# Sliding-window attention and a highway layer: scores in 64-column products, and three kinds of work moved between engines

## The chip, the cores and the metric

One core of a Trainium2 chip runs the whole kernel in one launch. The metric is the device time of one execution in microseconds, as the median of several runs. Engine names are those of the profile: PE is TensorE, with PEld its weight loads, DVE VectorE, ACT ScalarE, POOL GpSimd, and SP the queue that stores the results.

## The reference

Attention over 8 batches, 8 heads, 576 positions and head dimension 64, with a window of 128 positions backwards and a bias that falls linearly with distance, followed by a highway layer on the 4608 tokens of 512 features.

```python
scores = scale * np.matmul(q, k.transpose(0, 1, 3, 2))
bias = slopes[:, None, None] * (-np.abs(rel).astype(np.float32))[None, :, :]
mask = (rel >= 0) & (rel < window)            # rel = query position - key position
scores = np.where(mask, scores + bias[None], -1000000000.0)
attn = softmax(scores)                        # written out in the original
x = np.matmul(attn, v)                        # then heads side by side: (4608, 512)
H = np.maximum(x @ w_h, 0.0)
T = 1.0 / (1.0 + np.exp(-(x @ w_t + b_t)))
return (T * H + (1.0 - T) * x).astype(np.float32)
```

Inputs and output are float32; the kernel computes in bfloat16 with float32 sums.

## The kernel before

The attention is cut into 32 **units** (b, s, g): batch b, half s of the heads (four heads, whose two 32-wide halves of the head dimension stand on 32 partitions each), and half g of the sequence. The highway layer is cut into 36 **blocks** of 128 tokens: (b, 0) to (b, 3) for each batch, and (b, 4) on odd batches, which takes the first 64 tokens of two batches together.

Each kind of step has a letter. `L` loads q and k (line 105), v (111), weights and bias through POOL's queue, with a cast to bfloat16. `T` (line 156) transposes q or k of one half on DVE. `S` is set-up: relative positions on POOL and DVE, the masks `MT` by exp on ACT, the ones columns of v, the bias tile, `ident`. For each unit: `s` scores on PE (line 183), `e` exp on ACT (201), `m` the product with the mask `MT` on DVE (206), `p` the product with v on PE (214, 222 for the 64 first tokens, 234 for the neighbouring blocks), `n` division by the sum on DVE (247, 248). For each block: `x` transposes on PE (273), `c` copy on ACT (278), `h` the product with w_h (283), `u` relu minus x on DVE (288), `z` the product with w_t and the bias (296, 298), `a` tanh on ACT (302), `t` its scaling to a gate on ACT (306), `g` the product of gate and uu on DVE (310), `o` the sum with x on POOL (314), `d` the store on SP.

The order of all steps is a string written out by hand, `ORDER`; the digit behind s, p, x, h, z is the first of the PSUM banks it uses. All scores use banks 0 to 3, so the scores of a unit wait for the exp of the unit before; the other PE steps take turns on banks 4 to 7. Each engine takes its own instructions strictly in the order of the string and waits at each for the semaphores of what it needs. A load also waits for the load eight places before it.

A score step of a unit has 48 products, of 128 or 64 columns of weights (keys) by 128 or 64 queries, four at a time on four groups of 32 rows, and changes the shape of the tile inside the unit. The two 64-key neighbours of a block of 128 queries have products of their own:

```python
segs.append((P * i, P * i + D, P, 192 * o, 0, P))
...
segs.append((P * i + P, P * i + P, D, 192 * o + P, 0, D))
segs.append((P * i - D, P * i + D, D, 192 * o + P, D, D))
```

The memsets of set-up come last in it, in part 3, behind the relative positions, and the first loads of v stand before them in the string.

Of the kernel before, what the change touches and what calls it, by code (L numbers as in the profile page):

```python
# [9 lines left out]
P = 128  # L10
# [3 lines left out]

ORDER = (
    "LLLLLLSSSSLLLTLTLLs0LTLLLeLs0meTp4Lms0nep6LLnms0LeTp4LnLmx4x5cTp6Lz4nLs0atx6LTh4cez5uLTx"
    "4h7aLgcs0mcz5tuoeTz4Ldgp6aLmas0Lnp4eLh6noh7udx4Ts0cLx5tmh4cgex6uh5uLz7utmcs0LaTz6eLTp4oa"
    "ns0tdmp6ez4ngx5mp6cags0ntox4ez5TLdp6Tcos0anh4eLdTh5Lux6s0cuLz4meLTx5p6ams0cgh4tnoez5TLdp"
    "6utms0ah4egnoz5utLx6dmas0Lcx4gh5Teop6TLdcLs0tnLtz4egLup6oTh5aLdgtnos0z4uLdTx5x6Lch7maz5L"
    "cmeh4uLmp6aus0tnp4eggx6nh7ocp4touds0ndx6egz7gToh4amx5dcz7cTotz5aTLdp6aLgts0noh5euTx6Ldh4"  # L20
    "uz7cuz5matms0aTp6ex4nh5gcp6ms0uoz4neLdgx5mLp6aocs0nz4edmp6Tas0tnh4egx5oux6h7TcLdx4tz5uLc"
    "mtp6cmts0anh4egz5guop6Taodts0np4edmz6nx7map4cs0nx6gh7gToh4cez5uodup6Tdts0anx4x5mch6gz4uc"
    "oeTh5dx6uh7tas0ucz5gemz4op6tadgs0anoh5emdh4p6uttgus0onx5z4cdmtp6agox4nz5cdtgp6aotx4neh5d"
    "gh6oucz7udmz6ap4atx7nh6cgtx4gh5uocz7uodx6ah4gdcox5tz6gduz7oath4cdgaoz5uth4gdaotugdod"
# [3 lines left out]
def lists():  # L28

    units = [(b, s, g) for b in range(NB) for g in range(NG) for s in range(NS)]  # L30
    units[1], units[2] = units[2], units[1]
    blocks = []
    for b in range(NB):
        blocks += [(b, 0), (b, 1)] + ([(b, 4)] if b % 2 else []) + [(b, 2), (b, 3)]
    trs = [(b, s, w) for b in range(NB) for s in range(NS) for w in range(2)]
    loads = []
    for b in range(NB):
        for s in range(NS):
            loads += [("t", b, s, 0), ("t", b, s, 1)]
            if b < 2 or b % 2 == 0:  # L40
                n = 1 if b < 2 else 2
                loads += [("v", b, n, m) for m in ((0, 1, 2), (3, 4))[s]]
        if b == 0:
            loads += [("w", 0), ("w", 1), ("w", 2)]
    by = dict(L=loads, T=trs, S=list(range(4)))
    by.update({k: units for k in "sempn"})
    by.update({k: blocks for k in "xchuzatgod"})
    return by
# [3 lines left out]
def kernel(  # L52
# [10 lines left out]
    nc = tc.nc  # L63
# [17 lines left out]

    cp = ctx.enter_context(tc.tile_pool(name="const", bufs=1))
# [16 lines left out]
    REL = cp.tile([P, 448], F32, name="rel")  # L99
# [21 lines left out]
    def setup(part):  # L121
        if part == 0:
            rel = cp.tile([P, 448], I32, name="rel_i")
            far = cp.tile([P, 448], F32, name="far")
            for o in range(2):
                nc.gpsimd.iota(rel[:, 192 * o : 192 * o + 192], pattern=[[1, 192]], base=64,
                               channel_multiplier=-1)
                nc.gpsimd.iota(rel[0:D, 192 * o + P : 192 * o + 192], pattern=[[1, D]], base=0,
                               channel_multiplier=-1)
            nc.gpsimd.iota(rel[:, 384:448], pattern=[[1, D]], base=0, channel_multiplier=-1)  # L130
            nc.vector.tensor_copy(out=REL[:], in_=rel[:])
            nc.vector.tensor_scalar(out=far[:], in0=REL[:], scalar1=-63.5, scalar2=None,
                                    op0=ALU.add)
            nc.vector.tensor_tensor(out=far[:], in0=far[:], in1=far[:], op=ALU.mult)
            nc.vector.tensor_scalar(out=far[:], in0=far[:], scalar1=4096.0, scalar2=1.0e6,
                                    op0=ALU.is_gt, op1=ALU.mult)
            nc.vector.tensor_tensor(out=REL[:], in0=REL[:], in1=far[:], op=ALU.add)
        elif part < 3:
            s = part - 1
            for a in range(4):  # L140
                nc.scalar.activation(out=MT[s][:, a, :], in_=REL[:], func=ACTF.Exp,
                                     scale=-slopes[4 * s + a])
        else:
            for i in range(NB // 2):
                nc.vector.memset(VA[i][:, :, :, D:E], 1.0)
            nc.vector.memset(bT[:], 0.0)
            nc.vector.memset(ones0[:], 0.0)
            nc.vector.memset(ones0[0:1, :], 1.0)
            nc.vector.memset(ident[:], 1.0)
            nc.gpsimd.affine_select(  # L150
                out=ident[:], in_=ident[:], compare_op=ALU.is_equal, fill=0.0,
                base=0, pattern=[[1, P]], channel_multiplier=-1)
# [8 lines left out]
    PT, AV, X = {}, {}, {}  # L161

    def scores(b, s, g, bank):
        QT, KT = (TR[(4 * b + 2 * s + w) % NTR] for w in range(2))
        segs = []
        for o in range(2):
            i = 2 * g + o
            segs.append((P * i, P * i + D, P, 192 * o, 0, P))
        for o in range(2):
            i = 2 * g + o  # L170
            if i == 0:
                segs.append((P, P, P, P, 0, D))
            else:
                segs.append((P * i + P, P * i + P, D, 192 * o + P, 0, D))
                segs.append((P * i - D, P * i + D, D, 192 * o + P, D, D))
        if g == 0:
            segs.append((0, 0, P, 384, 0, D))
        first = True
        for k0, q0, m, col, row, n in segs:
            for e in range(2):  # L180
                for a in range(4):
                    rows = slice(32 * a, 32 * a + 32)
                    nc.tensor.matmul(  # L183
                        out=PS[row : row + m, bank + a, col : col + n],
                        lhsT=KT[rows, k0 : k0 + m, e], rhs=QT[rows, q0 : q0 + n, e],
                        start=first and e == 0, stop=e == 1, tile_position=(32 * a, row),
                        skip_group_check=True)
                first = False
# [5 lines left out]

    SB = {}
# [8 lines left out]
    def mask(b, s, g):  # L204
        p, w = PB[PT[b, s, g]], width(g)
        nc.vector.tensor_tensor(out=p[:, :, 0:w], in0=p[:, :, 0:w], in1=MT[s][:, :, 0:w],  # L206
                                op=ALU.mult)

    def pv(b, s, g, bank):
        AV[b, s, g] = bank  # L210
        me = PB[PT[b, s, g]]
        for o in range(2):
            for a in range(4):
                nc.tensor.matmul(  # L214
                    out=PS[:, bank + o, a * E : a * E + E], lhsT=me[:, a, 192 * o : 192 * o + P],
                    rhs=VA[b // 2][:, b % 2 * H + 4 * s + a, 2 * g + o, :],
                    start=a == 0, stop=False, skip_group_check=True)
        if g == 0 and b % 2:
            for a in range(4):
                for r in range(2):  # L220
                    at = 4 + a % 2
                    nc.tensor.matmul(
                        out=PS[r * D : (r + 1) * D, bank + a // 2, at * E : at * E + E],
                        lhsT=PB[PT[b - 1 + r, s, 0]][:, a, 384:448],
                        rhs=VA[b // 2][:, r * H + 4 * s + a, 0, :],
                        start=False, stop=True, tile_position=(0, r * D), skip_group_check=True)
        for o in range(2):
            i = 2 * g + o
            for a in range(4):
                for row, slot in ((0, i + 1), (D, i - 1)):  # L230
                    if slot < 0:
                        continue
                    orow = D - row
                    nc.tensor.matmul(  # L234
                        out=PS[orow : orow + D, bank + o, a * E : a * E + E],
                        lhsT=me[row : row + D, a, 192 * o + P : 192 * o + 192],
                        rhs=VA[b // 2][row : row + D, b % 2 * H + 4 * s + a, slot, :],
                        start=False, stop=True, tile_position=(row, orow), skip_group_check=True)
# [46 lines left out]

    def relu_sub(b, i):
        uu = UU[b, i] = ft.tile([P, DM], BF16, name="uu")
        nc.vector.scalar_tensor_tensor(  # L288
# [15 lines left out]
    def to_gate(b, i):  # L304
        tt = TT[b, i]
        nc.scalar.activation(out=tt[:], in_=tt[:], func=ACTF.Copy, bias=0.5, scale=0.5)  # L306

# [9 lines left out]
    def store(b, i):  # L317
# [5 lines left out]
        for r in range(2):  # L323
# [4 lines left out]
              h=mm_h, u=relu_sub, z=mm_z, a=tanh, t=to_gate, g=gate, o=add_x, d=store)  # L328
    by = lists()
    at = dict.fromkeys(by, 0)  # L330
    steps = iter("".join(ORDER))
    with tc.manual_schedule():
        for step in steps:
# [3 lines left out]
            if step in "spxhz":  # L337
                bank = int(next(steps))
                if step == "s":
                    SB[what] = bank  # L340
                what += (bank,)
            do[step](*what)
    assert all(at[i] == len(by[i]) for i in by)
# [29 lines left out]
```

## Time and profile before

| | us |
|---|---|
| median of 3 runs | 167.42 (167.25 to 167.76) |
| the profiled execution, its own time | 168.74 |
| its span, first to last instruction | 167.0 |
| PE, DVE, ACT, POOL busy | 134.0, 134.6, 111.2, 92.2 |
| granted TensorE clock, mean | 0.997 |

In the profile's lines, a group or a piece of the timeline names start, length, engine, line of the kernel, operation, tile written and read, shapes, how many instructions; in brackets behind it the idle time of the engine before, and what ended it. Busy times of neighbours on an engine overlap a little, so the time that an instruction really takes of its engine is the distance to the start of the next one where that does not wait.

### The profile page before, as it was taken

Reading aid. Unit: us, or ns where it says so; the run is one execution under the profiler, and the core shown is the slowest. Engines: PE = TensorE matmul, PEld = TensorE weight load, DVE = VectorE, ACT = ScalarE, POOL = GpSimd, SP = SyncE. Lnnn points to the kernel's source line nnn. Section 1 sums busy time; section 2 is a strip of 40 time slices with the busy share of each in tenths; the row PEclk is TensorE's granted clock in tenths of the full one; section 3 lists DMA queues with packets and bytes.
Section 4 is the critical chain, followed back from the end, with each engine's and each line's share of the span. In section 5 each row is a group of like instructions: output and inputs, shape, how many; then the busy total and the mean of one; then the engine's idle time right before and its main releaser. Section 6 shows DMA issues by size and latency. Waiting matters only on the chain.

```text
span 167.0 us, 6262 instructions
## 1 busy us (share of the span) xinstructions
PE 134.0 (80%) x2772; PEld 82.3 (49%) x2772; DVE 134.6 (81%) x213; ACT 111.2 (67%) x149; POOL 92.2 (55%) x106
## 2 busy tenths in 40 slices
PE   0002682999996988979999999999889999999960
PEld 0002561556654645646656465665556556655520
DVE  0357674869899899979999999999979978986560
ACT  3063642198598678669496977679766698687670
POOL 7609915759742593568965870825505233553752
PEclk9999999999999999999999999999999999999998
DMA  3977999999999999999999999296821113231443
GB/s 48 163 95 88 135 200 182 191 188 162 220 180 207 206 173 156 213 117 198 180 242 179 217 258 152 20 192 143 171 94 67 63 67 98 95 129 63 190 119 134
DMA packets 48235, 25.04 MB, mean 150 GB/s; under 512 B 38480, under 2 KB 39504, under 8 KB 48208
## 3 DMA queue, kind: packets, MB, share of 16 engines
q0 software_dynamic: 42960, 15.21, 83.9%
q1 hardware_dynamic: 5248, 9.44, 16.3%
q8 instruction: 21, 0.34, 0.8%
q14 instruction: 6, 0.05, 0.1%
HBM read 30.41 MB, written 9.44 MB: 239 GB/s over the span
## 4 chain that ended last, share of the span: by engine, by line
PE 49%; DVE 26%; DMA 10%; issue 7%; POOL 6%; POOLq 1%; DVEq 0%
PE ps L283 14%; PE ps L296 13%; PE ps L183 8%; DVE tr L156 7%; DMA ld<-in_q_dram 6%; DVE uu L288 5%; DVE p L206 5%; DVE x L248 5%; PE ps L273 4%; PE ps L234 4%; DMA va<-in_v_dram 4%; PE ps L298 3%; PE ps L214 3%; DVE uu L310 2%; POOL va L111 2%
## 5 line engine op out<-in xcount | busy, mean ns | idle before, releaser
L314 POOL TENSOR_TENSOR ot<-uu,x 128x512 f32<-128x512 bf16 x36 | 46.5, 1296 | 54.2 <-DVE uu L310 33.1
L201 ACT ACTIVATE p<-ps 128x1792 bf16<-128x1792 f32 (+1 forms) x32 | 49.9, 1560 | 19.0 <-PE ps L183 18.8
L183 PE MATMUL ps<-tr,tr 32*64 32x64 bf16 (+2 forms) x1536 | 26.8, 211 | 20.7 <-DVE tr L156 15.2
L156 DVE STREAM_TRANSPOSE tr<-ld 128x576 uint32<-128x576 uint32 x32 | 38.9, 1243 | 2.8 <-DMA ld<-in_q_dram 2.8
L296 PE MATMUL ps<-wT,xt 128*128 128x512 bf16 x144 | 38.0, 386 | 0.8 <-DVE uu L288 0.4
L283 PE MATMUL ps<-wH,xt 128*128 128x512 bf16 x144 | 36.2, 380 | 0.2 <-DVE x L248 0.2
L206 DVE TENSOR_TENSOR p<-p,mt 128x1792 bf16<-128x1792 bf16 (+1 forms) x32 | 32.2, 1013 | 2.3 <-ACT p L201 2.3
L183 PEld LDWEIGHTS <-tr 32*128 32x128 bf16 (+1 forms) x1536 | 19.5, 103 | 28.6 <-DVE tr L156 16.2
L278 ACT COPY xt<-ps 128x512 bf16<-128x512 bf16 x36 | 20.9, 586 | 14.4 <-PE ps L273 11.8
L288 DVE SCALAR_TENSOR_TENSOR uu<-ps,x 128x512 bf16<-128x512 f32 x36 | 24.2, 682 | 4.4 <-PE ps L283 3.1
L302 ACT ACTIVATE tt<-ps 128x512 f16<-128x512 f32 x36 | 21.4, 601 | 8.8 <-PE ps L298 8.6
L111 POOL DMA_DIRECT2D va<-in_v_dram x25 | 25.2, 1018 | 0.5 <-DMA va<-in_v_dram 0.4
L248 DVE TENSOR_TENSOR x<-ps,rd 128x512 bf16<-128x512 f32 (+1 forms) x32 | 24.3, 758 | 1.2
L306 ACT ACTIVATE tt<-tt 128x512 f16<-128x512 f16 x36 | 22.6, 634 | 0.2
L296 PEld LDWEIGHTS <-xt 128*128 128x128 bf16 x144 | 12.9, 99 | 14.9 <-issue 1.8
L310 DVE TENSOR_TENSOR uu<-uu,tt 128x512 bf16<-128x512 bf16 x36 | 16.3, 466 | 3.2 <-ACT tt L306 3.0
L283 PEld LDWEIGHTS <-xt 128*128 128x128 bf16 x144 | 12.7, 98 | 11.6 <-issue 0.3
L273 PE MATMUL ps<-ident,x 128*128 128x128 bf16 x144 | 14.0, 225 | 3.5 <-DVE x L248 3.4
L214 PEld LDWEIGHTS <-p 128*128 128x128 bf16 x256 | 12.0, 101 | 8.2 <-issue 3.2
L214 PE MATMUL ps<-va,p 128*128 128x65 bf16 x256 | 14.1, 200 | 2.2 <-issue 0.9
L234 PE MATMUL ps<-va,p 64*64 64x65 bf16 x448 | 14.9, 202 | 0.0
L273 PEld LDWEIGHTS <-x 128*128 128x128 bf16 x144 | 10.0, 100 | 8.7 <-DVE x L248 3.8
(31 smaller groups left out, 69.8 us busy)
## 6 DMA issues: line engine op xcount, KB each, us to landing
out_dram<-ot SPq DMA_DIRECT2D x32, 256.0 KB, 3.4
ld<-in_q_dram POOLq DMA_DIRECT2D x16, 288.0 KB, 8.5
ld<-in_k_dram POOLq DMA_DIRECT2D x16, 288.0 KB, 8.4
va<-in_v_dram POOLq DMA_DIRECT2D x12, 256.0 KB, 10.2
va<-in_v_dram POOLq DMA_DIRECT2D x11, 128.0 KB, 7.6
out_dram<-ot SPq DMA_DIRECT2D x8, 128.0 KB, 3.1
wH<-in_moe_w_h_dram POOLq DMA_DIRECT2D x1, 512.0 KB, 8.3
wT<-in_moe_w_t_dram POOLq DMA_DIRECT2D x1, 512.0 KB, 10.1
```

What stands on the lines that cost most here:

```text
L111: nc.gpsimd.dma_start(out=VA[b // 2][0:rows, h : h + n * H, m, 0:D], in_=v[b : b + n, :, m * P : m * P + rows].rearrange("b h p d -> p (b ...
L156: nc.vector.transpose(out=TR[i % NTR][:].rearrange("p s e -> p (s e)").bitcast(U32).rearrange("p (s t) -> p t s", t=NT), in_=LD[i % NLD][: ...
L183: nc.tensor.matmul(out=PS[row : row + m, bank + a, col : col + n], lhsT=KT[rows, k0 : k0 + m, e], rhs=QT[rows, q0 : q0 + n, e], start=firs ...
L201: nc.scalar.activation(out=PB[i][:, :, 0:w], in_=PS[:, bank : bank + 4, 0:w], func=ACTF.Exp, scale=scale)
L206: nc.vector.tensor_tensor(out=p[:, :, 0:w], in0=p[:, :, 0:w], in1=MT[s][:, :, 0:w], op=ALU.mult)
L214: nc.tensor.matmul(out=PS[:, bank + o, a * E : a * E + E], lhsT=me[:, a, 192 * o : 192 * o + P], rhs=VA[b // 2][:, b % 2 * H + 4 * s + a, ...
L248: nc.vector.tensor_tensor(out=X[b, g][:, s, :, 0:n, :], in0=av[:, :, 0:n, 0:D], in1=rd[:, :, 0:n, :].to_broadcast([P, 2, n, D]), op=ALU.mult)
L273: nc.tensor.transpose(out=XP[b, i][:, c * P : (c + 1) * P], in_=xchunk(b, i, c), identity=ident[:])
L283: nc.tensor.matmul(out=pa, lhsT=XT[b, i][:, c, :], rhs=wH[:, c, :], start=c == 0, stop=c == NC - 1)
L288: nc.vector.scalar_tensor_tensor(out=like(uu[:], i), in0=like(PA.pop((b, i)), i), scalar=0.0, in1=xview(b, i), op0=ALU.max, op1=ALU.subtract)
L296: nc.tensor.matmul(out=pz, lhsT=xt[:, c, :], rhs=wT[:, c, :], start=c == 0, stop=False)
L314: nc.gpsimd.tensor_tensor(out=like(ot[:], i), in0=like(UU.pop((b, i))[:], i), in1=xview(b, i), op=ALU.add)
```

## The change

The pieces of the probabilities are laid out anew: position j of a head's row holds 64 queries, rows 0 to 63 the keys of an even block of 64 and rows 64 to 127 those of the odd block before it. A block of 64 keys then meets 192 queries that lie side by side, and a score step is 40 products of 64 columns: 32 of up to 192 queries, 8 of 64. All have the tile shape of 32 rows by 64 columns. The product with v reads two tiles of probabilities in the second half of the sequence.

Seven units (`MASK_PE`) get their mask before the scores, as four products of a scaled identity `SI` with the relative positions `RB` into the same banks, and no `m` step. Twelve blocks (`RELU_ACT`) get a new step `r`, a relu on ACT from PSUM to a bfloat16 tile `rr`, and their `u` subtracts from that. Thirteen blocks (`GATE_DVE`) have `k`, a DVE step, in the place of `t`. Set-up begins with the memsets (and one of PSUM), the masks are made from 256 columns of positions in 16 exps, and a last part makes `SI` and `RB` on ACT. The loads of a batch come in another order, and `ORDER` is new throughout.

```diff
+RELU_ACT = (0, 1, 3, 5, 7, 8, 9, 12, 15, 20, 22, 24)
+GATE_DVE = (2, 3, 5, 6, 7, 9, 12, 15, 20, 26, 28, 29, 32)
+MASK_PE = (2, 3, 4, 6, 13, 16, 17)
...
-    "LLLLLLSSSSLLLTLTLLs0LTLLLeLs0meTp4Lms0nep6LLnms0LeTp4LnLmx4x5cTp6Lz4nLs0atx6LTh4cez5uLTx"
...
+    "SLLSSLLLTLLTLSLs0LLTeLLSTLms0Lp4eLms0nLp6eLLLnp4x6ns0cLTh4eLx5Tz6cLs0arLtup6egLh4nox5x6r"
...
-    units[1], units[2] = units[2], units[1]
...
+        if b == 0:
+            loads += ts[:2] + vs[:1] + ts[2:] + vs[1:3] + [("w", 0), ("w", 1), ("w", 2)] + vs[3:]
+        else:
+            loads += ts[:2] + vs[:3] + ts[2:] + vs[3:]
...
         if part == 0:
+            for i in range(NB // 2):
+                nc.vector.memset(VA[i][:, :, :, D:E], 1.0)
+            nc.vector.memset(PS[D:P, 0:4, 0:D], 0.0)
+            nc.vector.memset(bT[:], 0.0)
+            nc.vector.memset(ones0[:], 0.0)
+            nc.vector.memset(ones0[0:1, :], 1.0)
+            nc.vector.memset(ident[:], 1.0)
+        elif part == 1:
...
+        elif part == 4:
+            for h in range(H):
+                nc.scalar.activation(out=SI[:, h, :], in_=ident[:], func=ACTF.Copy,
+                                     scale=-slopes[h] / scale)
+            nc.scalar.copy(out=RB[:, 0:D], in_=REL[:, 192:256])
+            nc.scalar.copy(
+                out=RB[:, D:448].rearrange("p (o n) -> p o n", o=2),
+                in_=REL[:, 0:192].rearrange("p (o n) -> p o n", o=1).to_broadcast([P, 2, 192]))
...
     def scores(b, s, g, bank):
+        first = (b, s, g) not in by["pe_mask"]
+        if not first:
+            w = width(g)
+            for a in range(4):
+                nc.tensor.matmul(out=PS[:, bank + a, 0:w], lhsT=SI[:, 4 * s + a, :],
+                                 rhs=RB[:, 448 - w : 448] if g else RB[:], start=True,
+                                 stop=False, skip_group_check=True)
+        for i in (2 * g, 2 * g + 1):
+            lo, col = P * i, 192 * i - 448 * g
             for e in range(2):
+                for r in range(2):
+                    c0, c1 = col + r * D, col + r * D + 192
+                    q0 = lo + r * D
...
+                    for a in range(4):
+                        rows = slice(32 * a, 32 * a + 32)
+                        nc.tensor.matmul(
+                            out=PS[r * D : r * D + D, bank + a, c0:c1],
+                            lhsT=KT[rows, lo + r * D : lo + r * D + D, e],
+                            rhs=QT[rows, q0 : q0 + c1 - c0, e],
+                            start=first and e == 0, stop=e == 1, tile_position=(32 * a, r * D),
+                            skip_group_check=True)
...
+        t, col = (4, 384) if g == 0 else (8, 320)
...
+    def relu(b, i):
+        rr = RR[b, i] = fx.tile([P, DM], BF16, name="rr")
+        nc.scalar.activation(out=rr[:], in_=PA.pop((b, i)), func=ACTF.Relu)
+
     def relu_sub(b, i):
         uu = UU[b, i] = ft.tile([P, DM], BF16, name="uu")
+        if (b, i) in RR:
+            nc.vector.tensor_tensor(out=like(uu[:], i), in0=like(RR.pop((b, i))[:], i),
+                                    in1=xview(b, i), op=ALU.subtract)
+            return
...
+    def to_gate_v(b, i):
+        tt = TT[b, i]
+        nc.vector.tensor_scalar(out=tt[:], in0=tt[:], scalar1=0.5, scalar2=0.5, op0=ALU.mult,
+                                op1=ALU.add)
```

## Prediction

> **What bounds the kernel now.** I read the page first, for the balance of the engines.
>
> ```profile
> span 167.0 us, 6262 instructions
> PE 134.0 (80%) x2772; PEld 82.3 (49%) x2772; DVE 134.6 (81%) x213; ACT 111.2 (67%) x149; POOL 92.2 (55%) x106
> PE   0002682999996988979999999999889999999960
> DVE  0357674869899899979999999999979978986560
> PE 49%; DVE 26%; DMA 10%; issue 7%; POOL 6%; POOLq 1%; DVEq 0%
> ```
>
> The first line of busy times looks like an even load. The slices (4.2 us each) show two stages: up to slice 8 PE and DVE wait, after it both stand at 8 or 9. The chain that ended last (fifth line) passes PE for half of the span and DVE for a quarter. So there is a start that is paid in waiting, and a long stretch where PE is nearly full and DVE next to it.
>
> Then the timeline of the first 34 us, for what ends the waits of the start.
>
> ```profile
> 10.66 0.12 DVE L145 MEMSET va<- 128x80 bf16 x1 [1.07 <-DMA va<-in_v_dram]
> 12.65 0.29 POOL L150 TENSOR_SCALAR_AFFINE_SELECT ident<-ident 128x128 bf16<-128x128 bf16 x1 [5.66 <-DVE ident L149]
> 12.89 0.59 POOL L105 DMA_DIRECT2D ld<-in_k_dram  x1
> 14.83 1.23 PE L183 MATMUL ps<-tr,tr 32*128 32x128 bf16 x48 [14.83 <-DVE tr L156]
> 27.33 1.26 DVE L156 STREAM_TRANSPOSE tr<-ld 128x576 uint32<-128x576 uint32 x1 [2.55 <-DMA ld<-in_q_dram]
> 31.39 1.81 PE L296 MATMUL ps<-wT,xt 128*128 128x512 bf16 x4
> 33.36 0.82 PE L183 MATMUL ps<-tr,tr 32*128 32x128 bf16 x44
> ```
>
> The memset of the ones columns waits for the V load into the same tile; ident follows it; POOL stands 5.66 us for ident before it can issue the next load. So q and k of batch 0, landed at 5.7 and 7.5 us by the trace, are first used at 14.8, and q of batch 1 lands at 27.3 and is awaited. I call the score step of batch 1's first unit **the mark**: 33.36. Its predecessors there are the four units of batch 0, two x steps and one z step.
>
> Third, the stretch behind the mark: the table by stages for 33.35 to 161.5 (columns: window, length, busy time and instructions of PE, PEld, DVE, ACT, POOL), and the chain from 33 to 48 (start, length).
>
> ```profile
> 33.35:161.50 128.15, 121.79 (x2480) 73.55 (x2479) 115.16 (x180) 98.82 (x135) 70.40 (x71) 1.00 1.00 153
> 36.72 0.86 PE ps L283 x4
> 37.59 0.78 PE ps L183 x46
> 38.37 0.97 PE ps L296 x4
> 39.34 0.21 PE ps L298
> 41.49 0.62 PE ps L183 x42
> ```
>
> PE is busy 95% there, DVE 90%, ACT 77%, and the last PE work ends 5.5 us before the span does. What is worth time is therefore the start, and PE's own work behind the mark; DVE's work counts where PE waits for it.
>
> **PE's work behind the mark, before.** Per step, from chain pieces like these: h 0.86; z 0.86+0.22=1.08; x 0.22; scores 0.78 (g=0) or 0.62 (g=1), plus 0.11 that the next product starts later (0.97 against 0.86), so 0.89 and 0.73; pv 0.24+0.37 and the same 0.11, 0.73 with rounding, and 0.25 more for the eight extra pieces of an odd batch. Behind the mark stand 14 units of each kind, 28 pv (8 with pieces), 34 x, 36 h, 35 z: 22.7+22.4+7.6+31.0+37.8=121.5 us. The table says 121.8. So PE runs at 94.8% of its work's own length.
>
> **The change, part by part.**
>
> *Scores in 40 products.* All 40 keep one tile shape (32 rows, 64 columns), where before a unit switched shape inside. Four 32-row tiles run together already. The question is whether the two 64-column halves on the same rows do too. The nearest row is L222, 64-column halves of 128 rows, in a window of 20 ns:
>
> ```profile
> 40.81 0.22 PE L222 MATMUL ps<-va,p 128*64 128x65 bf16 x2
> ```
>
> Two products start within it, and the pair is over after 0.22 us, no longer than one (0.201 in the mean). In the chain the eight take 0.25 us to the next line's product, 0.12 of it the switch of shape: some 33 ns a pair, where 65 columns at L283's rate (0.216 us for 512) stream in 27. So the halves overlap, and I take eight score products as one wave of 192 columns: 0.081 us. Four waves, two short ones of 64 columns (0.027 each), 0.12 and 0.11 for the switches: 0.61 us, with rounding 0.62, for either g. Bounds: 0.62 where halves overlap, and 0.93 (g=0) or 0.82 (g=1) where they do not (eight waves at 0.081, or four and four at 0.054, and the rest as above). I take 0.62, since L222 is the same geometry in columns. 28 units: 17.4 against 22.7, **-5.3 us**.
>
> *Seven masks by TensorE.* Four products per unit, 448 or 384 columns: 4 x 0.189=0.76 or 0.65. Five lie behind the mark (four g=0, one g=1): **+3.7 us** of PE. They leave DVE's masks out: each 1.00 or 0.86 of DVE (here and below from one start to the next in the trace, since busy times of neighbours overlap), so -4.9 there.
>
> *Twelve relus on ScalarE.* DVE's relu step falls from 0.60 (f32 from PSUM) to what L310 shows for two bf16 operands, 0.33: -3.2 us of DVE. ACT gains 12 at L302's 0.48. *Thirteen gates on VectorE*: ACT loses 13 at L306's 0.52, DVE gains 13 at between 0.17 (half of L310: one operand in place of two) and 0.60 (L288); I take 0.2, as both operands are 16-bit in SBUF like L310's. DVE +2.6, at most +7.8. ACT ends 1.0 us lighter. A relu adds one engine to the path from h to uu, covered by the ft buffers and by PE's next products; bare, it is about 0.7 us each, 8 us in all.
>
> *Layout of the probabilities.* pv keeps its number of products. A g=1 unit now also reads its g=0 neighbour's tile, finished earlier: nothing.
>
> *Set-up and order.* Memsets come first and wait for nothing, so ident is there early and POOL issues on. Queue by queue: POOL issues q, k, three iotas and ident, then one v, q, k, v, v, wH, wT, bias, v, v, and q, k of batch 1. With the spacing of landings in this trace (q or k about 1.5 us, v 0.95, each weight 2.6, bias 0.1): k of the first half at 7.5, the second half's q, k at 9.9 and 11.4, the last v at 20.5, q and k of batch 1 at **22.0 and 23.4**, against 27.3 and 28.7. ACT's masks become 16 shorter exps, 4.7 us in all by L141's 3.84 for eight and one overhead more each; they end near 10, as the first scores do. The 10 small ACT copies for the TensorE masks (between 1.5 and 3 us) stand before the second unit's exp, which waits for its q and k anyway until 13.
>
> The last v at 20.5 lets pv of the third unit go. PE is at half clock by then, as it was at 31.39 (four z products 1.81 instead of 1.04 us). From 20.5: pv 1.2, x 0.4, masks and scores of the fourth unit 2.5, h 0.9, x 0.2, z 1.1, so 26.8; **the mark comes at 27.0** instead of 33.4, with one h more and one pv less done. Bounds: 25.5 if PE is warm, 29 if everything there runs at half clock. q and k of batch 1 are transposed by 24.6, before it.
>
> **The sum.** PE behind the mark: scores 17.4, masks 3.7, 29 pv 23.2, 34 x 7.6, 35 h 30.1, 35 z 37.8: 119.8 us. At the same 94.8% that is 126.4. DVE falls from 115.2 to about 109.5 busy behind the mark, so I give back a third of the 6.6 us that PE lost there: 124.4. End: 27.0+124.4+5.5 (the tail's steps are unchanged) = 156.9 span, 10.1 less than 167.0. The profiled execution took 168.74, so 1.74 lies around the span; the median of the runs is 167.42. 167.42-10.1 = **157.3 us**. The loads do not undo this: landings of batches 1 to 3 come about 5 us earlier and the steps that read them 6.4; by the new order there is 1 to 3 us between each landing and its transpose.
>
> **Rivals.**
> 1. *Loads carry on as the bound* (DMA is at 9 until slice 24): then only the 5.3 us by which q of batch 1 lands earlier are gained: 162.1. Against it: after 33 us only one transpose of before waits for a load, 0.25 us. Chance 0.12.
> 2. *The halves of the scores do not overlap*: +0.25 x 28/0.948=7.4, 164.7. L222 speaks against it. Chance 0.07.
> 3. *PE hardly waits* because DVE has slack: 98%, 122.2 instead of 124.4: 155.1. Chance 0.13.
> 4. *Slower: ScalarE's queue holds the scores.* All scores share four banks; each score step waits for the exp of the unit before, and relus now stand in ACT's queue waiting for h on PE. The nearest row is PE at L183 waiting for L201: 2.7 us in 3 waits, 0.9 each. It loses all the gain from 11 such waits among 28 units; at 18 it is 157.3+16.2=173.5. Against it: ACT is idle 23% behind the mark, mostly waiting for PE. Chance 0.05.
> 5. *Slower: each product takes a slot of its own.* L214's products, full tiles of 65 columns, start 30 ns apart (0.24 for eight). 40 such slots and the switches are 1.43 us, 0.81 more than 0.62: +23.9, 181.2. Against it: L183 now puts 48 products into 0.62, 13 ns each. Chance 0.01. The Trainium skill, TensorE: Matmul & The Clock Gate, section "Wait — 56ns, not 53.3ns?", states a rule of this kind: start to start never drops below about 25 ns however few columns. By it 40 products would need 1.0 us beside the switches, an estimate that makes 28 units 0.61 us each longer, about 175 us; the 13 ns row disagrees for tiles on different rows.
> 6. *The gains and costs cancel*, the kernel doing what it did: 0.02.
>
> **Numbers.** The forecast itself has 0.60. A measurement of this kernel tells about 0.3% from no change. Faster: 0.60+0.12+0.07+0.13=0.92; same 0.02; slower 0.06. The range goes from 152.5 (mark at 25.5 with rival 3 gives 153.6, with no wait at all 151.2) to 163.5 (mark at 29 and 94.8% give 161.3; gates at 0.6 add 5.2 us of DVE, of which PE would wait for less than half; rival 1 lies inside). Rivals 2, 4, 5 and 6, 0.15, stay out.
>
> **What would show it.** Right: first score near 8.7 us; POOL without a wait for ident; batch 1's first score at 25.5 to 29; a score step of 0.5 us up to the next product; PE 94 to 97% busy from the mark to its last product. Wrong: score steps near 0.8 (rival 2) or over 1.2 (5); transposes after 30 us behind loads (1); PE at the score line waiting for L236 exps over 10 us in sum (4); gates on DVE at 0.6; PE below 92% with none of these, which would be the order itself.

## The result, and the profile after

The changed kernel takes **161.86 us** (median of 4 runs, 160.85 to 162.73) against 167.59 for the kernel before on the same chip (4 runs, 167.25 to 170.28): a ratio of 0.966, 95% interval 0.959 to 0.974, or 5.7 us less. The forecast was 157.3, 10.1 us less. The profiled execution took 161.65 with a span of 159.9. All ratios below are to the kernel before, run beside the kernel on the same chip; they leave out runs that lie over 1.5% above the fastest of their kernel. Where a run is compared with the changed kernel in per cent, that is the quotient of the two ratios.

The page of the profile after, with the lines that answer to those shown of before (span, PE's busy time, the slices of PE, DVE and DMA, the chain that ended last):

```profile
span 159.9 us, 5790 instructions
PE 131.3 (82%) x2514; PEld 80.7 (50%) x2544; DVE 131.6 (82%) x220; ACT 113.6 (71%) x166; POOL 92.6 (58%) x104
PE   0027789999999995859989788999999999799960
DVE  4865452869999996988999797999999999988650
DMA  3999999999999999999999998759633122323343
PE 55%; DVE 22%; issue 8%; DMA 7%; POOL 4%; ACT 1%; POOLq 1%; DVEq 0%
```

PE stands at 7 or more from slice 4 on, where before it did so from slice 8 on, but in slices 16 and 18 it stands at 5, and at 7 or 8 in some up to slice 25: holes in the middle of the long stretch, under the 9s of the DMA line. "issue", time in which PE waited for nothing that the profile shows, is 8% of the chain.

The timeline of the start (start, length, engine and line; in brackets the idle time before and what ended it):

```profile
3.52 0.29 POOL L151 TENSOR_SCALAR_AFFINE_SELECT ident<-ident 128x128 bf16<-128x128 bf16 x1 [0.21 <-DVE ident L144]
8.42 0.86 PE L210 MATMUL ps<-tr,tr 32*64 32x192 bf16 x32 [8.42 <-DVE tr L181]
22.49 2.33 DVE L181 STREAM_TRANSPOSE tr<-ld 128x576 uint32<-128x576 uint32 x2
26.32 0.92 PE L195 MATMUL ps<-rb,si 128*128 128x448 bf16 x4
27.17 0.55 PE L210 MATMUL ps<-tr,tr 32*64 32x192 bf16 x32
```

POOL's wait for ident is 0.21 us in place of 5.66, the first scores run at 8.42, and the mark, which now begins with the masks by PE, comes at 26.32. So the start went as forecast. The table for the stretch from there to PE's last product shows where the rest stayed:

```profile
26.32:154.40 128.08, 118.81 (x2267) 72.16 (x2294) 115.46 (x190) 98.10 (x133) 72.67 (x72) 1.00 1.04 155
```

It is 128.1 us long, as long as before (128.15), where 124.4 was forecast. PE has its shorter work: 118.8 us in a trace that lacks 29 of the 2296 products, 119.8 and 120.3 in two traces below that have them all, 119.8 forecast. But DVE is busy for 115.5 us, as before, where I had put 109.5. PE's timeline in that stretch shows two kinds of holes.

```profile
63.24 0.25 PE L273 MATMUL ps<-va,p 64*64 64x65 bf16 x4 [1.58 <-issue]
68.54 0.40 PE L252 MATMUL ps<-va,p 128*128 128x65 bf16 x8 [0.90 <-DVE x L287]
70.81 0.42 PE L210 MATMUL ps<-tr,tr 32*64 32x128 bf16 x22 [1.02 <-issue]
```

The second waits for DVE's `x`. The first and third stand in the middle of a step, 12 products into a pv step and 10 into a score step, with no semaphore to wait for.

**Theory C, code loading.** Number the instructions of PE in program order, weight loads and products alike: the holes without a wait lie at places 1981, 2237, 3005 and 3261 in after and at 1473, 2241, 4033 and 4289 in before. That is 189, or 193, modulo 256 in every case. Two of those of before, as its timeline has them:

```profile
72.02 0.27 PE L183 MATMUL ps<-tr,tr 32*64 32x64 bf16 x11 [1.16 <-issue]
121.69 0.33 PE L183 MATMUL ps<-tr,tr 32*64 32x64 bf16 x28 [1.10 <-issue]
```

The queue that carries instructions moves pieces of 16384 bytes:

```profile
q8 instruction: 20, 0.33, 0.8%
```

20 of them for the 5088 weight loads and products of after, 21 for the 5544 of before, 19 in kernels with 5032: one for each such place in the program. So a piece is 256 instructions of 64 bytes, and PE stops at its boundary when the next one has not come. From the last weight load ahead of a boundary to the first behind it: 1.80, 1.29, 1.01 and 1.29 us, 5.4 in sum; in before 1.09, 1.38, 0.77 and 1.30, 4.5 in sum. The transfers belonging to the four of after ended 1.35 to 1.52 us before PE went on, and began 3.8 to 4.6 us after the boundary before; once the DMA line has fallen, behind 97 us, seven of eight begin at most 1.1 us after it, and no stop is seen. The Trainium skill, Runtime: NRT & Kernel Launch, section "Instruction fetch mechanics", gives the same blocks of 16 KiB, 256 instructions, fetched by a queue of their own while the block ahead runs, and calls the cost of crossing a boundary mostly hidden; the sizes agree with this trace, and the cost here, 5.4 us, was not hidden.

**Theory P, the port.** DVE's work does not shrink because GpSimd's add blocks it. DVE's groups, with mean ns of one, and two neighbours in the timelines of DVE and POOL:

```profile
L359 DVE TENSOR_SCALAR tt<-tt 128x512 f16<-128x512 f16 x13 | 6.8, 524 | 0.0
L241 DVE TENSOR_TENSOR p<-p,mt 128x1536 bf16<-128x1536 bf16 x13 | 14.1, 1081 | 0.0
L241 DVE TENSOR_TENSOR p<-p,mt 128x1792 bf16<-128x1792 bf16 x12 | 14.0, 1165 | 1.9 <-ACT p L236 1.9
```

```profile
64.95 1.21 POOL L368 TENSOR_TENSOR ot<-uu,x 128x512 f32<-128x512 bf16 x1 [6.65 <-issue]
65.06 1.25 DVE L359 TENSOR_SCALAR tt<-tt 128x512 f16<-128x512 f16 x1
```

Nine of the thirteen gates take 0.27 to 0.29 us. Three begin inside an add and take 0.92 to 1.25, until just behind its end; the fourth, 0.87 us at 48.53, begins while GpSimd issues a load of v (48.11, 1.18 us). Five of the 25 masks take 1.3 to 1.9 us in place of 0.95 or 1.08: four begin inside an add, one (78.85) beside the issue of a load of v. The other way round, a mask at 135.74 keeps its 0.95 us, and the add that begins inside it takes 1.75 us in place of 1.15. The Trainium skill, SBUF — State Buffer, section "Who interferes with whom", states this: DVE and GpSimd share a pair of ports, a DVE instruction with two SBUF inputs contends there with a GpSimd instruction that reads SBUF, one in a two-port mode contends with GpSimd, and whoever issues first blocks the other whole. The trace agrees, by the times above.

### The profile page after: what moved, and what is told of

It is laid out like the page before. It is cut to its first block, busy times and chain, and to the rows that moved or that the text cites. A ratio compares the mean times of both kernels' runs of the same rounds, so it can differ in the third digit from the quotient of the medians.

```text
span 159.9 us, 5790 instructions
## 1 busy us (share of the span) xinstructions
PE 131.3 (82%) x2514; PEld 80.7 (50%) x2544; DVE 131.6 (82%) x220; ACT 113.6 (71%) x166; POOL 92.6 (58%) x104
## 2 busy tenths in 40 slices
DMA packets 48234, 25.03 MB, mean 156 GB/s; under 512 B 38480, under 2 KB 39504, under 8 KB 48208
## 4 chain that ended last, share of the span: by engine, by line
PE 55%; DVE 22%; issue 8%; DMA 7%; POOL 4%; ACT 1%; POOLq 1%; DVEq 0%
PE ps L322 15%; PE ps L345 12%; DMA va<-in_v_dram 7%; PE ps L210 6%; DVE tr L181 6%; PE ps L273 6%; PE ps L252 5%; PE ps L312 4%; DVE x L287 4%; DVE p L241 4%; PE ps L347 3%; DVE uu L337 3%; PE ps L195 2%; DVE uu L364 2%; POOL va L126 2%
## 5 line engine op out<-in xcount | busy, mean ns | idle before, releaser
L368 POOL TENSOR_TENSOR ot<-uu,x 128x512 f32<-128x512 bf16 x36 | 47.4, 1319 | 56.2 <-DVE uu L364 32.7
L181 DVE STREAM_TRANSPOSE tr<-ld 128x576 uint32<-128x576 uint32 x32 | 39.4, 1245 | 2.1 <-DMA ld<-in_q_dram 1.4
L322 PE MATMUL ps<-wH,xt 128*128 128x512 bf16 x128 | 35.3, 380 | 1.3 <-issue 0.3
L345 PE MATMUL ps<-wT,xt 128*128 128x512 bf16 x130 | 35.3, 380 | 0.9 <-issue 0.3
L241 DVE TENSOR_TENSOR p<-p,mt 128x1536 bf16<-128x1536 bf16 (+1 forms) x25 | 28.0, 1121 | 1.9 <-ACT p L236 1.9
L210 PE MATMUL ps<-tr,tr 32*64 32x192 bf16 (+1 forms) x1024 | 18.3, 255 | 13.5 <-DVE tr L181 11.5
L351 ACT ACTIVATE tt<-ps 128x512 f16<-128x512 f32 x36 | 21.5, 598 | 10.1 <-PE ps L347 6.8
L210 PEld LDWEIGHTS <-tr 32*64 32x64 bf16 x1024 | 11.3, 110 | 21.5 <-DVE tr L181 12.0
L337 DVE SCALAR_TENSOR_TENSOR uu<-ps,x 128x512 bf16<-128x512 f32 x24 | 16.3, 683 | 4.1 <-PE ps L322 3.9
L364 DVE TENSOR_TENSOR uu<-uu,tt 128x512 bf16<-128x512 bf16 x36 | 15.0, 421 | 1.8 <-ACT tt L355 1.3
L355 ACT ACTIVATE tt<-tt 128x512 f16<-128x512 f16 x23 | 14.4, 632 | 0.2
```

Source lines behind the costliest of these rows:

```text
L181: nc.vector.transpose(out=TR[i % NTR][:].rearrange("p s e -> p (s e)").bitcast(U32).rearrange("p (s t) -> p t s", t=NT), in_=LD[i % NLD][: ...
L210: nc.tensor.matmul(out=PS[r * D : r * D + D, bank + a, c0:c1], lhsT=KT[rows, lo + r * D : lo + r * D + D, e], rhs=QT[rows, q0 : q0 + c1 - ...
L322: nc.tensor.matmul(out=pa, lhsT=XT[b, i][:, c, :], rhs=wH[:, c, :], start=c == 0, stop=c == NC - 1)
L345: nc.tensor.matmul(out=pz, lhsT=xt[:, c, :], rhs=wT[:, c, :], start=c == 0, stop=False)
L368: nc.gpsimd.tensor_tensor(out=like(ot[:], i), in0=like(UU.pop((b, i))[:], i), in1=xview(b, i), op=ALU.add)
```

## The experiments

**The parts alone.** First the start, on the kernel before:

```diff
-by = dict(L=loads, T=trs, S=list(range(4)))
+by = dict(L=loads, T=trs, S=[3, 0, 1, 2])     # memsets first; ident right behind the iotas; the new order of loads
-    "LLLLLLSSSSLLLTLTLLs0LTLLLeLs0me...
+    "SLLSSLLLTLLTLSLs0LLLLTLLLeLs0me...
```

> The kernel before with only the new set-up: memsets first, ident selected right behind the iotas, and the new order of the first loads; every other step, the old scores and the old order of steps stay. Theory A (the start is worth its own time, whatever follows): the first score falls from 14.8 us to near 8.5 and batch 1's first unit comes about 5 to 6 us earlier, so the time is near 161.5 us, about that of the changed kernel. Theory B (the changed kernel's gain was made by the shorter scores, and an earlier start alone is eaten by the loads): the loads of later batches hold the steps up and the time stays at 165 us or more.

Measured: 164.14 us, ratio 0.979 (0.973 to 0.985), 2.1% or some 3.5 us; first score at 9.2; the mark moves from 33.4 to 30.1 and the stretch behind it is 126.4 us. The time lies between the two theories, nearer to B's bound of 165. The mechanism is Theory A's, at a smaller size: the mark comes 3.3 us earlier in place of 5 to 6, and the stretch behind it does not grow, so the loads of later batches ate nothing. Then the scores, with the old start and the old order:

```diff
-MASK_PE = (2, 3, 4, 6, 13, 16, 17)   # likewise RELU_ACT, GATE_DVE
+MASK_PE = ()
-ORDER = (...)        # of after
+ORDER = (...)        # of before, with before's loads and order of set-up
```

> The old start and the old order of steps, with the new scores in 40 products and the new layout of the probabilities; no mask on TensorE, no relu on ScalarE, no gate on VectorE. Theory A (TensorE's work behind the mark counts): a score step falls from 0.89 or 0.73 us to about 0.62, 28 steps give 5.3 us, so about 162.5 us. Theory B (behind the mark the stretch is bound by more than TensorE's own work: it waits at instruction loads and for VectorE): half of it or less comes through, 165 to 167 us, and TensorE's busy time behind the mark falls by 5 us while its stretch hardly shortens.

Measured: 167.03 us, ratio 0.992 (0.987 to 0.996), 0.8% or 1.4 us, where PE's busy time behind the mark fell by 4.4 us (117.4). That is Theory B's time. The stretch in its profiled execution is 124.6 us, 3.5 less than before, but that execution (165.36 us) lies 1.7 below its median and that of before 1.3 above its own, so the stretch of the usual run shortens by less. And both together, still in the old order and with no work moved between engines:

```diff
-    S=list(range(5))    # and the three lists of moved work, now empty
+    S=list(range(4))    # new loads and order of set-up; ORDER of before behind start_alone's beginning
```

> The old order of steps with the new set-up and early loads and the new scores; no mask on TensorE, no relu on ScalarE, no gate on VectorE. The two parts alone gave 2.1% and 0.8%. If they add up, the ratio is near 0.971, and the moves between engines with the new order of steps are worth the remaining 0.5%. If the shorter scores are worth more once the start is earlier (the loads then lag), the ratio is 0.966 or less and the moves and the new order are worth nothing. If the moves are what makes the two work together, it is over 0.98.

Measured: 162.33 us, ratio 0.964 (0.959 to 0.969). That is as quick as the whole change (0.966). All of the gain is there without PE's masks, ACT's relus, DVE's gates and the new order. The two parts alone multiply to 0.971; that they give more together is not shown, as the difference lies within the intervals.

**The moves, each undone in the changed kernel.** Gates:

```diff
-              ..., t=to_gate, k=to_gate_v, ...
+              ..., t=to_gate, k=to_gate, ...
```

> The changed kernel with the thirteen gates back on ScalarE; nothing else differs. Theory P (VectorE's gates are held up by GpSimd's add and cost the gain): VectorE is busy 6.8 us less behind the mark, ScalarE 13 x 0.52 = 6.8 us more (to 82%), and the time falls by 1 to 3 us, to 159 to 161. Theory C (TensorE stands at instruction loads that VectorE's slack cannot give back): no change within 0.5%, the same stalls at the same program places. A third way: ScalarE's queue gets longer and the time rises by 1 us or more.

Measured: 161.39 us, ratio 0.962 (0.957 to 0.968): no change. DVE falls to 110.1 us behind the mark, ACT rises from 98.1 to 103.8, and the chain that ended last now has 7% of ACT where it had 1%. PE's waits for `x` fall from 2.4 to 1.3 us and the stretch from 128.1 to 127.3, but the mark comes at 27.4, 1.1 us later. The 1 to 3 us of Theory P did not come, and this run doesn't tell the theories apart. Masks and relus:

```diff
-        first = (b, s, g) not in by["pe_mask"]
+        first = True
...
+        if (b, s, g) in by["pe_mask"]:      # in soft, behind the exp
+            mask(b, s, g)
```

> The changed kernel without masks on TensorE: the seven units are masked by VectorE right behind their exp, like the others; the ten small set-up copies of the TensorE masks stay, unused. TensorE's work behind the mark falls by 3.7 us, VectorE's rises by 5 to 5.6 us. If TensorE's work alone sets the stretch: 3.5 us faster, about 158.3. If VectorE is as much the bound as TensorE (theory P): 1 to 3 us slower, 163 to 165, with VectorE over 95% busy. Theory C has the stalls at instruction loads move, since 28 instructions are gone from TensorE's program by the eighteenth unit.

Measured: 169.71 us, ratio 1.011 (1.005 to 1.017), 4.6% slower than the changed kernel, more than either theory said. The waits of PE in this kernel (us in total, times, longest):

```profile
PE ps L314 <- DVE x L289: 5.7, 4, 2.4
PE ps L254 <- DVE x L289: 4.2, 3, 2.7
```

DVE is busy for 120.5 of 135.6 us, 89% and not over 95, but `x` comes late to PE seven times, 9.9 us in all. The seven masks stand in one queue with the transposes and the divisions, right behind their exps, for which DVE waits 3.6 us too. So in the new order the 3.7 us of PE are well spent; whether masks on DVE at better places would cost as much is not shown.

```diff
-        rr = RR[b, i] = fx.tile([P, DM], BF16, name="rr")
-        nc.scalar.activation(out=rr[:], in_=PA.pop((b, i)), func=ACTF.Relu)
+        RR[b, i] = 1      # and here the scalar_tensor_tensor of the other blocks
```

> The changed kernel with the twelve relus back on VectorE, in one instruction with the subtraction, at the place where ScalarE's relu stood. VectorE gains 12 x (0.60 - 0.33) = 3.2 us, ScalarE loses 12 x 0.48 = 5.8 us busy. If VectorE sets part of the stretch (theory P): 1 to 2 us slower, 163 to 164. If the stretch is TensorE's with its instruction loads (theory C): no change within 0.5%.

Measured: 163.85 us, ratio 0.974 (0.968 to 0.981), 0.8% slower than the changed kernel, with intervals that overlap; on the side of Theory P and not enough for a verdict.

**Code loading.** If the stops belong to the program's places, they must not move with the work:

```diff
+            if n == 1:
+                for _ in range(64):
+                    nc.tensor.matmul(out=PS[:, 7, 0:64], lhsT=ones0[:], rhs=bT[:, 0:64],
+                                     start=True, stop=True, skip_group_check=True)
```

> The changed kernel with 64 unused products, each with its weight load, at the very start of TensorE's program, while it waits for the first transposes; they write a bank that is overwritten later. So every later instruction of TensorE stands 128 places further on in its program. Theory C (TensorE stops at each 256th instruction until its next 16 KB of program have come): the gaps without a wait, at places 189 mod 256 now, stay at the same places counted from the program's start, that is, they come 128 instructions earlier in the work; the time may move by up to 1 us either way, as the stops meet other work. Rival (the gaps belong to the steps they stand in, by a bank, a tile or a port): they stay with the same steps of the work. The first score should not be later than 8.4 us by more than 0.5.

Measured: 161.18 us, ratio 0.958 (0.952 to 0.965), not to be told from after.

```profile
68.27 0.30 PE L210 MATMUL ps<-tr,tr 32*64 32x128 bf16 x9 [1.66 <-issue]
93.33 0.27 PE L210 MATMUL ps<-tr,tr 32*64 32x192 bf16 x3 [0.88 <-issue]
```

Its stops are again at 189 modulo 256 (the longest at 1725, 2237, 3261: 1.0, 2.0 and 1.2 us from weight load to weight load), that is, 128 instructions earlier in the work. The pv step that stopped for 1.8 us at 61.4 runs through. The rival is out. Next, the loads:

```diff
+            if b >= 5:      # q and k
+                return
+            if b >= 4:      # v; the steps read VA[b // 2 % 2]
+                return
```

> The changed kernel without the loads of q and k for the last three batches and of v for the last four; those batches work on what the tiles held before, so the output is not the reference's. The transfers that fill the DMA engines until about 100 us end earlier, near 65 us. Theory C with its condition (the stops of TensorE are instruction loads that stand in line behind the loads of data): the stops at the 256th instructions vanish behind that point, the two at 89.4 and 95.4 us among them, and the time falls by 2 to 3 us. Rival (the stops do not depend on the DMA queues' load): they stay as long, and the time falls only by what waits for loads cost there, under 1 us.

Measured: 158.58 us, ratio 0.944 (0.936 to 0.951). Slices of the DMA engines, the table from the mark to PE's end, and the one stop that is left:

```profile
DMA  3999999999999995021330120141213114233243
```

```profile
26.30:150.75 124.45, 120.32 (x2296) 72.06 (x2294) 115.03 (x190) 97.89 (x133) 56.01 (x50) 1.00 0.56 112
```

```profile
62.27 0.25 PE L277 MATMUL ps<-va,p 64*64 64x65 bf16 x4 [0.78 <-issue]
```

The DMA engines are at 9 until slice 15 and at 5 in slice 16, which ends at 62.5 us. The stop at 61.3 shrinks from 1.8 to 1.0 us, the three behind it are gone, and the stretch is 3.6 us shorter although DVE is as busy as ever. Theory C holds with its condition.

**The port.** First GpSimd's add left out:

```diff
-        ot = OT[b, i] = ft.tile([P, DM], F32, name="ot")
-        nc.gpsimd.tensor_tensor(...)
+        UU.pop((b, i))
+        OT[b, i] = OC
```

> The changed kernel without GpSimd's final add: a constant tile is stored in its place, so the output is not the reference's; the stores stay, released earlier. Theory P: VectorE's stretched instructions vanish (gates 13 x 0.28 in place of 0.52, masks 1.0 at most), VectorE's busy time behind the mark falls by 6 us or more, to 109 or less, and the stretch shortens by 2 to 4 us. Theory C: VectorE's busy time falls the same, but TensorE keeps its stops of 1 to 1.8 us, and the end moves by less than 1 us, apart from the tail, which loses the last add (1 to 1.5 us).

Measured: 181.96 us, ratio 1.066. The time says nothing of the theories: stores of a constant tile wait for nothing, so all 9.4 MB went out first and held the loads up; the mark came at 51.4. From there on the run can be read:

```profile
51.40:174.60 123.20, 119.78 (x2296) 72.11 (x2294) 109.74 (x190) 97.78 (x133) 28.75 (x38) 1.00 0.94 95
```

DVE is busy for 109.7 us, the 109.5 of the prediction, and the stretch is 4.9 us shorter. Stops of 0.7 to 1.2 us at places 1981, 2237, 3005 and 3261 are still there. But a late start lets other work catch up, so it was done again with the stores' waits kept:

```diff
-        nc.gpsimd.tensor_tensor(out=like(ot[:], i), in0=like(UU.pop((b, i))[:], i), in1=xview(b, i), op=ALU.add)
+        nc.gpsimd.tensor_tensor(out=ot[:, 0:4], in0=UU.pop((b, i))[:, 0:4], in1=..., op=ALU.add)
```

> The changed kernel with GpSimd's final add cut to 4 of 512 columns, written into four constant tiles that are stored in turn, so the output is not the reference's; order, waits and stores stay as they are. Theory P: VectorE's gates fall from 0.52 to 0.28 us, its masks by 0.1 us each, VectorE's busy time behind the mark from 115.5 to 109 to 110.5, and the stretch from the mark to TensorE's end shortens by 2 to 4 us; TensorE keeps its stops at every 256th instruction, and the tail loses about 1 us with the last add. If VectorE's slack is worth nothing to TensorE: the stretch stays within 1 us although VectorE's busy time falls.

Measured: 159.47 us, ratio 0.942 (0.936 to 0.947), 2.5% or 4.1 us less than after by the two ratios (the medians, each taken beside other runs of before, lie 2.4 apart), 0.9 of it in the tail. The three groups of DVE:

```profile
L361 DVE TENSOR_SCALAR tt<-tt 128x512 f16<-128x512 f16 x13 | 3.7, 282 | 0.0
L243 DVE TENSOR_TENSOR p<-p,mt 128x1536 bf16<-128x1536 bf16 x13 | 12.3, 950 | 0.0
L243 DVE TENSOR_TENSOR p<-p,mt 128x1792 bf16<-128x1792 bf16 x12 | 13.0, 1084 | 1.9 <-ACT p L238 1.8
```

No gate takes over 0.29 us and no mask over 1.1; DVE's busy time behind the mark is 110.0. PE's three waits for `x` (1.1, 0.8 and 1.2 us in after, from weight load to weight load) are gone; the stops without a wait stay. In the profiled execution (160.99 us) they even add up to 6.7 us, one of them 3.1, at a granted clock of 0.97 in the stretch, which is 128.4 us long there: that the stretch shortens stands on the times and on the run without the add, not on this trace. The short add also sets GpSimd free earlier, but in after neither PE nor DVE has a wait of over 0.2 us for it behind the mark. So both theories hold, side by side, and each is worth some 3 to 4 us.

**Giving the code its turn.** If the instructions stand in line behind data that is not needed yet, loads issued later should free them. In after, loads of batch 4 land 9.6 to 13.3 us after their issue, and those of q and k 9 us or more ahead of their transposes. Only the `L`s move in `ORDER`:

```diff
-    "...6egLh4nox5x6rz7TcLdp4atLTz7cLns0h6euz4u..."
+    "...6egh4noLx5x6rz7TcdLp4atTz7cnLs0h6euLz4u..."
```

> The changed kernel with the loads from batch 2 on issued later in the order: each at the step that runs when the load two before it has landed, so two or three are in flight instead of five to eight; everything else keeps its order. The DMA engines stay busy and the loads should land within 2 us of where they do now, still 1 to 8 us ahead of their transposes. Theory C, sharpened (each 256 instructions of TensorE need 16 KB of program, which are asked for when the piece before is begun and which stand in line behind the data already queued: 4.6 us from the boundary at 56.2 to the start of the transfer at 60.8, 0.3 us at 116.6 when the queues are short): the wait in line shrinks to 1 to 3 us, TensorE's stops behind the mark fall from 5.4 us to under 2, and the time falls by 2 to 4 us, to about 158.5 to 160. Rival (the wait depends on the DMA engines being busy at all, not on how much is queued): the stops stay at 4 to 6 us and the time within 1 us; if transposes then wait for loads, it is slower by 1 to 3 us.

Measured: six runs, two at 159.64 and 160.64 us and four at 164.1 to 165.3, median 164.25; the ratio, 0.952 (0.946 to 0.959), is by the rule above that of the first two. In the profiled execution (160.64 us) the stops at the four places of after are 0.2 to 0.5 us; one of 0.9 is new, at 43.2. Its transposes of batch 3 come 0.02 to 0.8 us after the landings, so there is nothing left when a load is late. None of the four longer runs was profiled, and what held them up stays open. Hence the same from batch 4 on only:

```diff
-    "...5cLgz4LaToth5amLdrs0Lkegp6uuz4ons0Ldamh5eTLx4p6cgs0..."
+    "...5cLgz4aToth5amdrs0kegp6uuz4ons0damh5eTx4Lp6cgs0..."
```

> The changed kernel with the loads issued later from batch 4 on only (batches 2 and 3 keep their places, since with all of them moved the transposes of batch 3 had 0.02 to 0.8 us left and only two of six runs were quick): two in flight for batch 4, three for batch 5, and 2.8 us or more between the loads of batches 6 and 7. Every load should land 2 us or more ahead of its transpose. Theory C: TensorE's stops at 61, 70, 89 and 95 us fall from 5.4 us in sum to under 2, and all runs, not some, take 158.5 to 160.5 us, ratio 0.945 to 0.957. Rival (the transfers of data set the pace as well, so that what the stops give back is lost in waits for loads or for VectorE): 161 to 163 us, ratio 0.962 to 0.972, no better than the changed kernel.

Measured: **159.23 us** (six runs, 157.25 to 160.19), ratio 0.938 (0.930 to 0.945), below the interval of the changed kernel: 3.0% less by the two ratios, 2.6 us by the medians. It is the quickest version here that computes all; the old order with the same care for the loads was not run.

```profile
66.66 0.40 PE L252 MATMUL ps<-va,p 128*128 128x65 bf16 x8 [0.90 <-DVE x L287]
83.08 0.40 PE L252 MATMUL ps<-va,p 128*128 128x65 bf16 x8 [1.44 <-DVE x L287]
```

These are PE's only waits of over 0.6 us between 50 and 100 us: the stops at boundaries fell from 5.4 to 0.5 us, the waits for `x` stayed. The code's transfers for the four places of after began 2.7, 4.2, 1.4 and 0.4 us after the boundary before, in place of 4.6, 4.1, 4.0 and 3.8. The stretch from the mark (26.7) to PE's end is 124.9 us, 3.1 less, with the DMA engines as full as before (at 9 until slice 26, 24 in after): what counted was how much is queued ahead of the code, not how much is moved in all.

## Why the prediction was right and where it failed

- **The start**: right. First score 8.42 (near 8.7 forecast), q and k of batch 1 transposed from 22.5 on, the mark at 26.3 against 27.0.
- **Score steps**: right, rivals 2 and 5 are out. A step takes 0.53 us up to the next product (27.17 to 27.70), 0.62 forecast; halves of 64 columns on the same rows run together, and 40 products take 13 ns each.
- **Gates at 0.2, DVE down to 109.5**: failed as a term. The gate by itself is 0.28 us, but four of thirteen cost up to 1.25, and masks are stretched too: 115.5 in place of 109.5. The seven masks lightened DVE by 2.3 us (28.1 to 25.9) in place of 4.9. The bound of 7.8 us for thirteen gates held their 6.8; I took the low end by the usual time of the nearest row, L310. The blocking cost some 3 us by the run with the short add. L310's longest instruction in the trace of before already shows it, 1.38 us in place of 0.41, begun inside an add:

```profile
56.34 1.93 POOL L314 TENSOR_TENSOR ot<-uu,x 128x512 f32<-128x512 bf16 x1 [5.38 <-DVE uu L310]
57.18 1.38 DVE L310 TENSOR_TENSOR uu<-uu,tt 128x512 bf16<-128x512 bf16 x1
```

- **"Give back a third of the 6.6 us that PE lost there"**: this is the step that failed. Of the 6.6 us, 4.5 were stops at code boundaries, which no slack of DVE returns; 2.1 remained. In the changed kernel the stops are 5.4 and the waits for `x` 3.1. PE lost 8.3 us (128.1 against 119.8) where 4.6 were forecast, so that its work filled some 94% of the stretch. (A third of 6.6 is 2.2 and makes 124.2; the sum gave back 2.0.)
- **The tail**: 5.5 us, as forecast.
- **The base of the sum**: the profiled execution of before (168.74) lay 1.3 us above its median, that of after (161.65) did not. By spans, 167.0 to 159.9, the gain is 7.1 us against 10.1 forecast: 0.7 better at the mark, 3.7 worse behind it. The other 1.3 us of the miss is this.
- **Rival 1** (loads carry on as the bound) gave 162.1 and came out nearest in number, by another mechanism: no transpose waits for data; PE waits for its code behind the data. **Rival 3** is out by the 8.3 us that PE lost. **Rival 4** is out: behind the mark the score line of PE has no wait for an exp among its longer ones. The range, 152.5 to 163.5, held the result by its width: its upper end came from a late mark and slow gates, not from the code.

Not settled: what the new order and the three moves would be worth with both costs gone. Against the old order without them, 0.964, they add nothing here.

## What to carry to other kernels

Before slack of another engine is credited to TensorE, split its lost time by what ended it: gaps inside a step, with nothing to wait for, at places of the program that repeat every 256 instructions, were code loading here, and were shortened by issuing data loads only as early as they were needed. Work moved to VectorE is priced beside GpSimd's work of the same stretch, not by its quiet rows: look at the spread of a group, not at its mean. And a part that takes 4 to 5 us off an engine's work may return 1.4 alone; run the parts alone and together before crediting the moves around them.

## What the runs showed that I had not expected

- Stops of TensorE of 0.8 to 1.8 us in before and after, up to 3.2 in another kernel's trace (relus_dve), at those 256th instructions where the next 16 KB had begun to move only some 3 to 5 us after the boundary before. With short queues in after the transfer mostly began within some 1 us and no stop was seen.
- A short DVE instruction on 16-bit data (0.28 us alone) that begins inside a GpSimd add waits to the add's end: 1.25 us. One that began beside the issue of a load by GpSimd took 0.87.
- Two versions with the same DMA load in all, 25.03 MB, differ by 4.9 us in TensorE's stops, by the places of the loads in the order alone.
